# Moving the DRAM copies of queries and keys: four later places in the beginning, eight places in the middle stretch

## The chip, the cores and the metric

The kernel runs on one core of a Trainium2 chip. The metric is the device time of one launch in microseconds. A core has TensorE (PE; its weight loads are PEld), VectorE (DVE), ScalarE (ACT), GpSimd (POOL) and SyncE (SP). Each works through its own instructions in order. SP does nothing here but issue transfers; POOL issues some too. All transfers share 16 DMA engines.

## The reference, cut to what matters

Three layers follow one another. Attention looks back over a window of 64 positions; its 4 batches of 576 positions and 8 heads of 64 become 2304 tokens of width 512. A gated layer multiplies two products of the tokens. A mixture layer lets 32 slots collect the tokens, sends the slots through 8 experts and gives the result back to the tokens.

```python
scores = scale * np.matmul(q, k.transpose(0, 1, 3, 2))      # q, k, v: (4, 8, 576, 64)
mask = (rel >= 0) & (rel < 64)
attn = softmax(np.where(mask, scores, -1e9))
x = np.matmul(attn, v)                                      # as 2304 tokens x 512
x = (x @ w_a) * (x @ w_b) @ w_out                           # 512 -> 1536 -> 512
logits = x @ phi                                            # 32 slots
d = softmax(logits, over tokens); slot_input = d.T @ x
slot_out[e] = relu(slot_input[e] @ w1[e]) @ w2[e]           # 8 experts, 4 slots each
out = softmax(logits, over slots) @ slot_out
```

## The kernel before

The tokens are worked in 18 tiles of 128. For each tile attention makes scores (`att_s`), divides them by their sums (`att_n`), turns them (`att_pt`) and multiplies with the values (`att_pv`, tile `xps`). Then the gated layer (`glu`) makes three column groups of 512; each group is two products of 12 matmuls, in the PSUM banks `psa` and `psb`, and ACT copies `psa` out (L505) before the next `psa` may start. The products of the gated layer are then turned and multiplied with the projected slot weights (`r_b` and `r_l`), and the mixture layer's sums run along (`r_k`, `r_d`, `r_u`).

Much of the turning is done by way of DRAM. `r_b` turns 32x32 squares on DVE (`gq`), writes four pieces to DRAM (`gd`, L552) and reads them back in another order (`gT`, L557), all from SP's queue; `r_l` uses `gT` on TensorE (tile `lps` or `ups`, L573). From tile 7 on `att_pt` does the same with the scores from POOL's queue: `pq` on DVE, four writes `pd` (L374), two reads `pT` (L380), which `att_pv` needs.

Queries and keys of tiles 9 and up (`NTURN`) come turned as well: `relay_part` (L211) copies a quarter of one batch's queries or keys from the input to a DRAM tensor `dq` or `dk`, 2304 runs of 32 numbers, and `load_turned` (L205) reads from there. A batch's queries are four such copies, its keys another four. Batch 2 begins with tile 9, batch 3 in the middle of tile 13. So there are 16 copies, and all 16 are in the beginning.

The work has two stretches. The beginning, tiles 0 to 4 and parts of 5 and 6, follows the string `STARTUP`, in which each word is the next piece of one function; within it every engine's order is that of the string. `Xq2` is the next copy of batch 2's queries, `Xk3` the next of batch 3's keys. `Po` is a piece of `project_phi`, which reads and decodes `w_out` (L427 on ACT, L429 to L439 on DVE), turns it on TensorE (tile `two`) and writes it back from POOL (`wo_dram`, L701). `Sa`, `Sb`, `Da` and `Db` read and decode the gated layer's weights.

After that come slots 30 to 107, one slot for each product of the gated layer, with `events` that hang further work on a slot (`at(slot, function, ...)`). There only TensorE's order is that of the program. The order on the other engines, SP among them, is chosen when the program is compiled, by a planner that works with durations of its own; it may also take instructions of these slots ahead of the last words of `STARTUP`. Slot 46 holds `att_s` of tile 9 and `load` of tile 10's queries and keys, slot 64 the load of tile 13's.

Of the kernel before, what the change touches and what calls it, by code (L numbers as in the profile page):

```python
# [34 lines left out]
    Da1.1 Po1 Gb1.0 As3 Da1.1 Gb1.0 Po1 Gb1.0 Ga1.0 An3.0 Po1 Sb1.0 As4 Av2 As4 Ak5 Po1 Po1 Ga2.0 Sb1.1  # L35
    Sa1.0 An3.0 Da1.1 Gb1.0 Sb1.1 An3.1 An3.0 Po1 As4 Po1 Aq5 Da1.0 Ga2.0 Ga2.0 Ap3.1 Ap3.1 Tq5 Da1.1 Ap3.0 Tv3
    Da1.0 Da1.0 Po2 Ap3.0 Tv3 Db1.0 Ga2.0 Da1.0 Gb2.0 Ak5 Av3 Ak5 Da1.0 Gb2.0 Gb2.0 Av3 Av3 Gb2.0 Db1.0 Ga2.0
    Po2 Ga3.0 Ga3.0 Da1.0 As4 Ga3.0 Gb2.0 Ga3.0 Tq6 Xq2 Xk2 Da1.0 Aq6 Db1.0 Ga3.0 Tv4 Gb3.0 Ga0.1 As4 Db1.0
    Sa2.1 Po2 Ga0.1 Db1.0 Po2 Sa2.1 Tq6 Xq2 Xk2 Xq2 Ga0.1 Gb3.0 As4 Ga0.1 Db1.0 Po2 Po2 Po2 An4.0 An4.0
    An4.1 Tv4 As5 Db1.0 Ga0.1 Gb3.0 Po1 Po2 Sb2.0 Ga2.1 An4.0 Ga2.1 Po2 Gb3.0 Po4 Po2 As5 Po2 Gb3.0 Aq6  # L40
    Db1.1 Db1.1 Ga2.1 Po2 Db1.1 Ga2.1 Db1.1 Ap4.1 Po2 Ga2.1 Gb2.1 Ap4.1 Ap4.0 Po2 Ap4.0 Db1.1 Po4 Po2 Db1.1 Ga1.1
    Db1.1 Po4 Ga1.1 Po2 Sb2.0 Ga1.1 Po4 Po4 Gb2.1 Po4 Av4 Sa2.0 Ga1.1 Gb2.1 Ga1.1 Po2 Sa2.0 Da2.0 Gb2.1 Po4
    Gb2.1 Av4 As5 Ga3.1 Da2.0 Ga3.1 Po4 Da2.0 Da2.0 Av4 Po4 Po5 Ga3.1 Gb3.1 Gb3.1 Da2.0 Po4 Po4 Po4 Ga3.1
    As5 Po4 Ga3.1 Ak6 Gb3.1 Gb3.1 Po4 Gb3.1 Ak6 Po5 Da2.0 Ga4.1 Da2.0 Po4 Ga4.1 Po5 As5 Po4 Po5 Po4
    Po5 Ga4.1 Ga4.1 Gb1.1 Gb1.1 Po5 Ga4.1 Po5 Gb1.1 Ga4.0 Gb1.1 As5 Ga4.0 Da2.1 Ak6 Gb1.1 Da2.1 Ga4.0 Po5 Ga4.0
    Tv5 Po5 An5.0 Po5 An5.0 Gb4.0 Da2.1 Ga4.0 Da2.1 Gb4.0 Po5 Sb2.1 Gb4.0 Da2.1 Sb2.1 Da2.1 Po5 Gb4.0 Po5 Gb4.0
    Ga3.2 An5.0 Ga3.2 Po5 An5.1 Db2.1 Da2.1 Gb0.1 Gb0.1 Ap5.0 Db2.1 Ga3.2 Ga3.2 Db2.1 Db2.1 Ap5.1 Po5 Db2.1 Po5 Gb0.1
    Tv5 Xk2 Xq2 Xk2 Ga3.2 Ga2.2 Gb0.1 Gb0.1 Ap5.1 Db2.0 Ga2.2 Db2.1 Ga2.2 Db2.0 Ga2.2 Gb4.1 Db2.0 Db2.0 Gb4.1 Gb4.1
    Ap5.0 Ga2.2 Db2.0 Db2.1 Po3 Db2.0 Ga0.2 Po3 Xq3 Xk3 Xq3 Xk3 Ga0.2 Gb4.1 Ga0.2 Gb4.1 Po3 Ga0.2 Db2.0 Po3
    Av5 Po3 Gb2.2 Gb2.2 Gb2.2 Po3 Po3 Ga0.2 Ga4.2 Po5 Gb2.2 Gb2.2 Ga4.2 Po3 Po3 Po3 Ga4.2 Gb0.2 Po3 Po3  # L50
    Po3 Gb0.2 Gb0.2 Tv6 Ga4.2 Av5 Gb0.2 Ga4.2 Po3 Po3 Ga1.2 Gb0.2 Po3 Av5 Gb3.2 Gb3.2 Rt0.0 Gb3.2 Rt0.0 Gb3.2
    Rt0.1 Rt0.1 Rt0.2 Po3 Ga1.2 Rt0.2 Gb3.2 Gb4.2 Rl0 Gb4.2 Rl0 Rk0 Gb4.2 Rk0 Gb4.2 Ga1.2 Rk0 Rk0 Gb4.2 Rk0
    Ga1.2 Rk0 Ga1.2 Gb1.2 Rd0 Gb1.2 Gb1.2 Gb1.2 Rd0 Gb1.2 Tv6 Xq3 Xk3 Xq3 Xk3 Ru0 Ru0
"""
MANUAL = {mybir.EngineType.PE}
QUEUES = {mybir.EngineType.PE, mybir.EngineType.DVE, mybir.EngineType.Activation, mybir.EngineType.Pool, mybir.EngineType.SP}
# [8 lines left out]
def swa_glu_softmoe_kernel(  # L65
# [13 lines left out]
    nc = tc.nc  # L79
    B, H, S, D = q.shape  # L80
# [108 lines left out]
    def runs(t0, n):  # L189
        done = 0  # L190
        while done < n:
            b, s = divmod(t0 + done, S)
            step = min(n - done, S - s)
            yield done, step, b, s
            done += step
# [11 lines left out]
    def relay_part(nm, b, i, d):  # L207

        src = (q if nm == "q" else k)[b].rearrange("h s d -> (h s) d")
        n = H // 2 * S  # L210
        nc.sync.dma_start(  # L211
            out=d.rearrange("a (j e) -> a j e", e=32),
            in_=src[n * (i // 2):n * (i // 2) + n, 32 * (i % 2):32 * (i % 2) + 32].rearrange("(j a) e -> a j e", a=32),
        )

    def relay(nm, b):

        d = turned[nm, b] = dram.tile([4, 32, H // 2 * S], F32, name=f"d{nm}{b}")
        for i in range(4):
            relay_part(nm, b, i, d[i])  # L220
            yield

    def load(t, names="qkab"):
        tiles = loaded.setdefault(t, {})
        for nm, src, t0 in (("q", q, P * t), ("k", k, P * t), ("a", v, P * t - W), ("b", v, P * t)):
# [3 lines left out]
            o = 0  # L229
            if nm in "qk" and t >= NTURN:  # L230
                for off, n, b, s in runs(t0, P):
# [21 lines left out]
    def att_q(t):  # L253
        if t >= NTURN:
            x = loaded[t]["q"].rearrange("p h d -> p (h d)")
            nc.scalar.activation(out=x, in_=x, func=ACTF.Copy, scale=-SCALE)
            yield
            qT = qTs[:, t % 2]
            nc.vector.transpose(out=qT.rearrange("p u s -> p (u s)"), in_=x)
            sts[t] = {"qT": qT}  # L260
            return
        tq = ps_t.tile([P, 4, P], F32, tag="t", name="tq")
        x = loaded[t]["q"]
        for u in range(4):
            transpose(tq[:, u], x[:, 2 * u:2 * u + 2].rearrange("p h d -> p (h d)"))
        yield
        qT = qTs[:, t % 2]
        nc.scalar.activation(out=qT, in_=tq, func=ACTF.Copy, scale=-SCALE)
        sts[t] = {"qT": qT}

    def att_k(t):
# [5 lines left out]
        yield  # L277
        if t >= NTURN:
            x = loaded[t]["k"].rearrange("p h d -> p (h d)")
# [114 lines left out]
    def att_pv(t):  # L394
        st = sts[t]
        xps = ps_t.tile([P, 4, P], F32, tag="x", name="xps", bufs=1)
        for b in range(2):
            vt = loaded[t]["b" if b else "a"]
            c = slice(W * b, W * b + W)
            for n in range(H):  # L400
                h, u = divmod(n, 4) if t >= NTURN else (n % 2, n // 2)
                o = xps[W * (n % 2):W * (n % 2) + W, n // 2, c]
# [444 lines left out]
    def at(n, f, *a):  # L847
        events[round(4 * n) if n > NSLOT - 3 else 2 * round(2 * n)].append((f, a))
# [58 lines left out]
    a, b, c = LAST  # L907
# [203 lines left out]
    with tc.manual_schedule(engines=MANUAL | {mybir.EngineType.Activation, mybir.EngineType.DVE}):  # L1111
# [57 lines left out]
```

## Time and profile before

| | us |
|---|---|
| median of 3 runs | 526.72 |
| lowest, highest | 524.45, 527.68 |
| the profiled execution, device time | 524.64 |
| its span, first to last instruction | 522.7 |
| mean granted TensorE clock over the span | 0.973 |

The profiled execution has 1.94 us outside its span. TensorE is busy in 92% of the span, DVE in 58%, ACT in 37%. In timelines a line gives start, duration, engine, line of the kernel, operation, tile written and tiles read, how many, and in brackets how long the engine sat idle before and what ended that.

### The profile page before, as it was taken

What the parts mean: (1) busy time and instruction counts of PE and PEld (TensorE: products, weight loads), DVE (VectorE), ACT (ScalarE), POOL (GpSimd) and SP (SyncE); (2) the same over time, 40 slices, a digit from 0 to 9 for tenths busy, and PEclk for the clock granted to TensorE, in tenths of its full rate; (3) what the DMA queues carried; (4) which work ended last, traced back from release to release, by engine and by line L of the source; (5) the groups of instructions that cost most, each with busy time, mean ns of one, the idle gap of its engine ahead of it and who ended that gap; (6) DMA issues with size and microseconds to landing.
All of it is one profiled execution on the core that took longest, in us unless ns stands there. A gap on an engine that the chain in (4) does not pass through costs nothing.

```text
span 522.7 us, 10423 instructions
## 1 busy us (share of the span) xinstructions
PE 482.2 (92%) x3911; PEld 355.6 (68%) x3911; DVE 300.7 (58%) x759; ACT 193.1 (37%) x586; POOL 64.8 (12%) x136
## 2 busy tenths in 40 slices
PE   3769999999699969999999999999999999999993
PEld 2547777778477746777777777877777777743352
DVE  4989796896614543847667485677673211151133
ACT  4877765733421401324424143334432211231022
POOL 4101000000000020111130211212243000020000
PEclk9798999999799979999999999999999999999998
DMA  9999999589804186789877777875679999799998
GB/s 262 293 287 288 280 217 315 162 194 190 167 2 108 35 205 157 185 223 213 229 182 196 194 171 208 229 195 151 192 208 266 323 349 374 254 367 391 383 344 287
DMA packets 164898, 121.22 MB, mean 232 GB/s; under 512 B 102512, under 2 KB 141936, under 8 KB 164848
## 3 DMA queue, kind: packets, MB, share of 16 engines
q1 hardware_dynamic: 160112, 105.87, 72.1%
q0 software_dynamic: 4736, 14.68, 9.4%
q8 instruction: 31, 0.51, 0.4%
q14 instruction: 19, 0.16, 0.1%
HBM read 95.88 MB, written 29.36 MB: 240 GB/s over the span
## 4 chain that ended last, share of the span: by engine, by line
PE 70%; DMA 18%; ACT 4%; DVE 3%; SPq 2%; issue 1%; POOL 0%; DVEq 0%; POOLq 0%; ACTq 0%
PE psb L498 26%; PE psa L498 25%; DMA xw<-in_moe_w_dram 7%; PE xps L408 3%; PE ups L676 2%; DMA ldk<-in_k_dram 2%; PE s L317 2%; DMA ldb<-in_v_dram 2%; ACT pr L337 2%; DMA gd<-gq 2%; PE ups L573 1%; DMA st<-in_moe_w_out_dram 1%; PE tg L140 1%; PE two L140 1%; DMA pT<-pd 1%
## 5 line engine op out<-in xcount | busy, mean ns | idle before, releaser
L498 PE MATMUL psa<-wa,x 128*128 128x512 f32 x648 | 170.7, 405 | 5.8 <-ACT g L505 5.1
L498 PE MATMUL psb<-wb,x 128*128 128x512 f32 x648 | 169.0, 403 | 0.0
L498 PEld LDWEIGHTS psa<-wa,x 128*128 128x128 f32 x648 | 120.0, 192 | 33.8 <-ACT g L505 5.3
L498 PEld LDWEIGHTS psb<-wb,x 128*128 128x128 f32 x648 | 119.3, 191 | 27.6 <-issue 3.1
L510 DVE TENSOR_TENSOR g<-psb,g 128x512 f32<-128x512 f32 (+1 forms) x54 | 36.4, 676 | 62.9 <-PE psb L498 61.4
L505 ACT COPY g<-psa 128x512 f32<-128x512 f32 x53 | 30.9, 583 | 81.7 <-PE psa L498 75.7
L337 ACT ACTIVATE pr<-pr,nmx 128x128 f32<-128x128 f32 x96 | 37.2, 389 | 21.5 <-DVE nmx L330 21.5
L546 DVE STREAM_TRANSPOSE gq<-g 128x512 f32<-128x512 f32 x42 | 29.2, 703 | 8.0 <-DMA gd<-gq 7.4
L374 POOL DMA_DIRECT2D pd<-pq x44 | 24.2, 558 | 73.0 <-DVE pq L367 67.7
L358 DVE TENSOR_TENSOR pr<-pr,rs 128x512 f32<-128x512 f32 x36 | 24.4, 683 | 0.7
L609 ACT ACTIVATE e<-lt,nm 128x128 f32<-128x128 f32 x17 | 6.2, 365 | 49.7 <-DVE nm L605 46.9
L411 ACT CAST x<-xps 128x512 fp32r<-128x512 f32 x18 | 10.5, 585 | 37.2 <-PE xps L408 37.2
L276 POOL COPY kTs<-kTs 128x256 f32<-128x256 f32 x17 | 7.9, 463 | 122.8 <-DVE kTs L291 49.6
L317 PE MATMUL s<-kTs,qTs 64*64 64x128 f32 x576 | 21.9, 293 | 0.0
L330 DVE CUSTOM_DVE_ANT_0 pr<-s,masks 128x128 f32<-128x128 f32 x80 | 17.6, 285 | 7.1 <-PE s L317 7.1
L380 POOL DMA_DIRECT2D pT<-pd x22 | 16.5, 756 | 38.4 <-DMA pd<-pq 34.1
L317 PEld LDWEIGHTS s<-kTs,qTs 64*64 64x64 f32 x576 | 17.2, 144 | 5.8 <-issue 5.2
L337 ACT ACTIVATION_READ_ACCUMULATOR pr<-pr,nmx 128x1 f32 x96 | 17.9, 186 | 0.0
L337 ACT ACTIVATE pr<-s,nmx 128x128 f32<-128x128 f32 x48 | 17.0, 378 | 1.8 <-DVE nmx L327 1.8
L413 DVE TENSOR_TENSOR x<-xps,x 128x512 fp32r<-128x512 f32 x18 | 12.3, 685 | 8.9 <-ACT x L411 8.9
L701 POOL DMA_DIRECT2D wo_dram<-wo x6 | 4.5, 754 | 102.2 <-DVE wo L439 76.4
L427 ACT ACTIVATE w<-st 128x1024 f32<-128x1024 f32 (+1 forms) x14 | 14.3, 1023 | 7.2 <-DMA st<-in_moe_w_a_dram 3.8
(155 smaller groups left out, 602.3 us busy)
## 6 DMA issues: line engine op xcount, KB each, us to landing
xw<-in_moe_w_dram SPq DMA_DIRECT2D x46, 512.0 KB, 6.6
gd<-gq SPq DMA_DIRECT2D x168, 64.0 KB, 2.9
gT<-gd SPq DMA_DIRECT2D x42, 256.0 KB, 3.1
xw<-in_moe_w_dram SPq DMA_DIRECT2D x27, 256.0 KB, 7.2
st<-in_moe_w_b_dram SPq DMA_DIRECT2D x12, 512.0 KB, 6.1
st<-in_moe_w_out_dram SPq DMA_DIRECT2D x12, 512.0 KB, 5.5
st<-in_moe_w_a_dram SPq DMA_DIRECT2D x12, 512.0 KB, 7.2
pd<-pq POOLq DMA_DIRECT2D x44, 128.0 KB, 3.5
```

The source lines that it names most:

```text
L317: nc.tensor.matmul(sps[h][c, u], lhsT=qT[r, u, c], rhs=kTs[r, t % 2, u, W * b:W * b + P], start=not early, stop=not early or u == 3,)
L330: nc.vector.tensor_tensor_reduce(out=pr[:, u].rearrange("p (a k) -> p a k", a=2), in0=sps[h][:, u].rearrange("p (a k) -> p a k", a=2), in1 ...
L337: nc.scalar.activation(out=pr[:, u], in_=sps[h][:, u] if early else pr[:, u], func=ACTF.Exp, scale=-1.0, bias=nmx[:, i:i + 1], accum_out=s ...
L358: nc.vector.tensor_tensor(out=pr, in0=pr, in1=rs.to_broadcast([P, 4, P]), op=ALU.mult)
L374: nc.gpsimd.dma_start(out=pd[:, :, i].rearrange("j k e -> k j e"), in_=pq[32 * i:32 * i + 32].rearrange("p j h u q -> p j (h u q)"),)
L380: nc.gpsimd.dma_start(out=pT, in_=pd[:, :, :, P * h:P * h + P].rearrange("j k i e -> (j k) i e"))
L408: nc.tensor.matmul(o, lhsT=vt[:, n, :], rhs=r)
L427: nc.scalar.activation(out=t, in_=hi.bitcast(F32), func=ACTF.Abs)
L498: nc.tensor.matmul(ps, lhsT=l[:, kk], rhs=r, start=(n == 0), stop=(n == 3 * KD - 1))
L505: nc.scalar.copy(out=pas[t, fg], in_=ps)
L510: nc.vector.tensor_tensor(out=g[:, c:c + step], in0=ps[:, c:c + step], in1=pa[:, c:c + step], op=ALU.mult)
L546: nc.vector.transpose(out=gq.rearrange("p (j c t) -> p c j t", j=4, c=4), in_=gts[t][:, 512 * fg:512 * fg + 512].rearrange("p (c j f) -> p ...
```

## The change

Nothing that is computed changes, and there are 16 copies as before. In `STARTUP` the first pair of copies is taken out, the next three words are batch 2's first three (`Xq2 Xk2 Xq2`), of the next three words one is left (`Xk2`), the four words that copied batch 3 copy the rest of batch 2, and the four words at the end are taken out. Batch 3's eight copies hang on slots 46, 48, ... 60, queries and keys in turn. Each is put directly behind the SP instruction that was traced last before it (`keep_in_program_order`).

```diff
-... Ga3.0 Tq6 Xq2 Xk2 Da1.0 Aq6 Db1.0 ...
+... Ga3.0 Tq6 Da1.0 Aq6 Db1.0 ...
 ... Sa2.1 Tq6 Xq2 Xk2 Xq2 Ga0.1 ...
-... Tv5 Xk2 Xq2 Xk2 Ga3.2 ...
+... Tv5 Xk2 Ga3.2 ...
-... Db2.0 Ga0.2 Po3 Xq3 Xk3 Xq3 Xk3 Ga0.2 ...
+... Db2.0 Ga0.2 Po3 Xq2 Xk2 Xq2 Xk2 Ga0.2 ...
-... Gb1.2 Tv6 Xq3 Xk3 Xq3 Xk3 Ru0 Ru0
+... Gb1.2 Tv6 Ru0 Ru0
+    LATER = 46
-        nc.sync.dma_start(
+        return nc.sync.dma_start(
         for i in range(4):
-            relay_part(nm, b, i, d[i])
-            yield
+            yield relay_part(nm, b, i, d[i])
+    relays = {}
+    def relay_late(nm, b):
+        if (nm, b) not in relays:
+            relays[nm, b] = relay(nm, b)
+        tc.keep_in_program_order(next(relays[nm, b]))
+    for n in range(8):
+        at(LATER + 2 * n, relay_late, "qk"[n % 2], B - 1)
```

## Rows read from the trace of the kernel before

**Rows 1.** The page, part 1: engine, busy us, share of the span, instructions.
```profile
PE 482.2 (92%) x3911; PEld 355.6 (68%) x3911; DVE 300.7 (58%) x759; ACT 193.1 (37%) x586; POOL 64.8 (12%) x136
```

**Rows 2.** Windows: from:to, length, busy us by engine (instructions), PEclk, DMA share, GB/s.
```profile
20.00:59.00 39.00, 32.72 (x354) 24.24 (x351) 35.74 (x54) 29.28 (x83) 2.34 (x4) 0.96 1.07 290
59.00:131.00 72.00, 70.93 (x488) 55.23 (x491) 58.13 (x70) 38.57 (x81) 3.00 (x5) 1.00 0.89 221
130.00:163.00 33.00, 27.92 (x189) 21.09 (x187) 13.87 (x41) 10.59 (x33) 0.72 (x1) 0.90 0.40 78
177.00:201.00 24.00, 16.59 (x138) 11.99 (x135) 12.03 (x42) 5.96 (x24) 3.72 (x6) 0.86 0.66 155
234.00:292.00 58.00, 57.42 (x506) 44.28 (x502) 39.64 (x139) 20.68 (x82) 11.31 (x19) 1.00 0.83 205
```

**Rows 3.** Timeline of SP: three of the 16 copies, and tile 13's queries.
```profile
60.91 3.41 SPq L211 DMA_DIRECT2D dk<-in_k_dram  x1
...
119.84 0.55 SPq L211 DMA_DIRECT2D dq<-in_q_dram  x1
...
135.38 1.88 SPq L211 DMA_DIRECT2D dk<-in_k_dram  x1
...
297.95 1.21 SPq L205 DMA_DIRECT2D ldq<-dq  x2
```

**Rows 4.** DMA from 134 to 138 us, when copies alone were in flight.
```profile
DMA packets 4927, 0.63 MB, mean 156 GB/s; under 512 B 4927, under 2 KB 4927, under 8 KB 4927
```

**Rows 5.** Timeline of TensorE: its idle times from 59 to 190 us.
```profile
92.24 0.66 PE L140 MATMUL two<-ident,wo 128*128 128x128 f32 x4 [1.07 <-DVE wo L439]
...
130.91 1.10 PE L317 MATMUL s<-kTs,qTs 64*64 64x128 f32 x32
137.10 1.65 PE L498 MATMUL psa<-wa,x 128*128 128x512 f32 x3 [5.08 <-ACT g L505]
...
186.12 0.49 PE L593 MATMUL lt<-l,ri 128*128 128x128 f32 x2 [4.14 <-DVE l L583]
```

**Rows 6.** Timeline of ACT: what stands ahead of two copies TensorE waits for.
```profile
87.08 1.13 ACT L427 ACTIVATE wo<-st 128x1024 f32<-128x1024 f32 x1 [2.40 <-DMA st<-in_moe_w_out_dram]
...
132.38 0.40 ACT L337 ACTIVATE pr<-pr,nmx 128x128 f32<-128x128 f32 x1 [6.64 <-DVE nmx L330]
...
135.47 1.10 ACT L427 ACTIVATE wo<-st 128x1024 f32<-128x1024 f32 x1
136.48 0.56 ACT L505 COPY g<-psa 128x512 f32<-128x512 f32 x1
```

**Rows 7.** Timeline of POOL: the reads of turned scores, tiles 9, 10 and 11.
```profile
248.56 1.50 POOL L380 DMA_DIRECT2D pT<-pd  x2 [3.30 <-DMA pd<-pq]
...
271.31 1.50 POOL L380 DMA_DIRECT2D pT<-pd  x2 [3.61 <-DMA pd<-pq]
...
293.28 1.50 POOL L380 DMA_DIRECT2D pT<-pd  x2 [3.46 <-DMA pd<-pq]
```

**Rows 8.** Timeline of TensorE: where those reads and `gT` are used.
```profile
255.33 0.69 PE L408 MATMUL xps<-pT,lda 128*64 128x64 f32 x16
...
261.07 0.84 PE L573 MATMUL ups<-gT,wphi 128*32 128x128 f32 x24
...
277.98 0.69 PE L408 MATMUL xps<-pT,lda 128*64 128x64 f32 x16
...
300.08 0.69 PE L408 MATMUL xps<-pT,lda 128*64 128x64 f32 x16
```

**Rows 9.** Landing: of `pT`, 234 to 300; issues with KB and median, 234 to 292.
```profile
DMA to landing us min/median/max: 3.6/4.2/4.7
...
gT<-gd SPq DMA_DIRECT2D x12, 256.0 KB, 3.1
gd<-gq SPq DMA_DIRECT2D x48, 64.0 KB, 3.0
```

**Rows 10.** Timeline of SP: the last `gT` read of tile 6.
```profile
253.89 0.34 SPq L557 DMA_DIRECT2D gT<-gd  x1
```

**Rows 11.** Issues by tile, median landing: 106 to 113 us, then 140.8 to 146.
```profile
wo_dram<-wo POOLq DMA_DIRECT2D x1, 512.0 KB, 7.0
...
wo_dram<-wo POOLq DMA_DIRECT2D x1, 512.0 KB, 4.5
```

More of the change, by code (lines that the diff above doesn't have):

```diff
@@ L37 @@
     Da1.0 Da1.0 Po2 Ap3.0 Tv3 Db1.0 Ga2.0 Da1.0 Gb2.0 Ak5 Av3 Ak5 Da1.0 Gb2.0 Gb2.0 Av3 Av3 Gb2.0 Db1.0 Ga2.0
[L38 to L51, printed above, removed]
@@ L52 @@
-    Rt0.1 Rt0.1 Rt0.2 Po3 Ga1.2 Rt0.2 Gb3.2 Gb4.2 Rl0 Gb4.2 Rl0 Rk0 Gb4.2 Rk0 Gb4.2 Ga1.2 Rk0 Rk0 Gb4.2 Rk0
-    Ga1.2 Rk0 Ga1.2 Gb1.2 Rd0 Gb1.2 Gb1.2 Gb1.2 Rd0 Gb1.2 Tv6 Xq3 Xk3 Xq3 Xk3 Ru0 Ru0
+    Po2 Ga3.0 Ga3.0 Da1.0 As4 Ga3.0 Gb2.0 Ga3.0 Tq6 Da1.0 Aq6 Db1.0 Ga3.0 Tv4 Gb3.0 Ga0.1 As4 Db1.0 Sa2.1 Po2
+    Ga0.1 Db1.0 Po2 Sa2.1 Tq6 Xq2 Xk2 Xq2 Ga0.1 Gb3.0 As4 Ga0.1 Db1.0 Po2 Po2 Po2 An4.0 An4.0 An4.1 Tv4
+    As5 Db1.0 Ga0.1 Gb3.0 Po1 Po2 Sb2.0 Ga2.1 An4.0 Ga2.1 Po2 Gb3.0 Po4 Po2 As5 Po2 Gb3.0 Aq6 Db1.1 Db1.1
@@ new lines @@
+    Ga2.1 Po2 Db1.1 Ga2.1 Db1.1 Ap4.1 Po2 Ga2.1 Gb2.1 Ap4.1 Ap4.0 Po2 Ap4.0 Db1.1 Po4 Po2 Db1.1 Ga1.1 Db1.1 Po4
+    Ga1.1 Po2 Sb2.0 Ga1.1 Po4 Po4 Gb2.1 Po4 Av4 Sa2.0 Ga1.1 Gb2.1 Ga1.1 Po2 Sa2.0 Da2.0 Gb2.1 Po4 Gb2.1 Av4
+    As5 Ga3.1 Da2.0 Ga3.1 Po4 Da2.0 Da2.0 Av4 Po4 Po5 Ga3.1 Gb3.1 Gb3.1 Da2.0 Po4 Po4 Po4 Ga3.1 As5 Po4
+    Ga3.1 Ak6 Gb3.1 Gb3.1 Po4 Gb3.1 Ak6 Po5 Da2.0 Ga4.1 Da2.0 Po4 Ga4.1 Po5 As5 Po4 Po5 Po4 Po5 Ga4.1
+    Ga4.1 Gb1.1 Gb1.1 Po5 Ga4.1 Po5 Gb1.1 Ga4.0 Gb1.1 As5 Ga4.0 Da2.1 Ak6 Gb1.1 Da2.1 Ga4.0 Po5 Ga4.0 Tv5 Po5
@@ new lines @@
+    An5.0 Po5 An5.0 Gb4.0 Da2.1 Ga4.0 Da2.1 Gb4.0 Po5 Sb2.1 Gb4.0 Da2.1 Sb2.1 Da2.1 Po5 Gb4.0 Po5 Gb4.0 Ga3.2 An5.0
+    Ga3.2 Po5 An5.1 Db2.1 Da2.1 Gb0.1 Gb0.1 Ap5.0 Db2.1 Ga3.2 Ga3.2 Db2.1 Db2.1 Ap5.1 Po5 Db2.1 Po5 Gb0.1 Tv5 Xk2
+    Ga3.2 Ga2.2 Gb0.1 Gb0.1 Ap5.1 Db2.0 Ga2.2 Db2.1 Ga2.2 Db2.0 Ga2.2 Gb4.1 Db2.0 Db2.0 Gb4.1 Gb4.1 Ap5.0 Ga2.2 Db2.0 Db2.1
+    Po3 Db2.0 Ga0.2 Po3 Xq2 Xk2 Xq2 Xk2 Ga0.2 Gb4.1 Ga0.2 Gb4.1 Po3 Ga0.2 Db2.0 Po3 Av5 Po3 Gb2.2 Gb2.2
+    Gb2.2 Po3 Po3 Ga0.2 Ga4.2 Po5 Gb2.2 Gb2.2 Ga4.2 Po3 Po3 Po3 Ga4.2 Gb0.2 Po3 Po3 Po3 Gb0.2 Gb0.2 Tv6
@@ L54 @@
+    Ga4.2 Av5 Gb0.2 Ga4.2 Po3 Po3 Ga1.2 Gb0.2 Po3 Av5 Gb3.2 Gb3.2 Rt0.0 Gb3.2 Rt0.0 Gb3.2 Rt0.1 Rt0.1 Rt0.2 Po3
+    Ga1.2 Rt0.2 Gb3.2 Gb4.2 Rl0 Gb4.2 Rl0 Rk0 Gb4.2 Rk0 Gb4.2 Ga1.2 Rk0 Rk0 Gb4.2 Rk0 Ga1.2 Rk0 Ga1.2 Gb1.2
+    Rd0 Gb1.2 Gb1.2 Gb1.2 Rd0 Gb1.2 Tv6 Ru0 Ru0
 """
```

## The prediction, made before the changed kernel was run

> **What bounds the kernel now.** The page comes first: TensorE is busy in 92% of the span [rows 1], so a change pays only where TensorE waits. The copies are issued by SP from about 60 us to 137 us [rows 3], so I read the windows of that stretch and of the slots that receive the copies [rows 2]. From 59 to 131 us TensorE is busy 70.93 of 72 us at full clock. The DMA engines have a share of 0.89 there and look like the bound; they aren't. From 234 to 292 us TensorE is busy 57.42 of 58 us, and the DMA share is already 0.83. In the full stretch from 20 to 59 us it reached 1.07, which I take as the ceiling (a share is the sum of packet times, and packets overlap).
>
> Next I looked for TensorE's idle times in its timeline. From 59 to 190 us three are over 1 us [rows 5]: 1.07 us ahead of 92.24, 5.08 ahead of 137.10, 4.14 ahead of 186.12. The last two come with a lower granted clock: the window from 130 to 163 has 0.90, the one from 177 to 201 has 0.86, so part of each ran at 1.2 GHz instead of 2.4 [rows 2]. The reader should see that the copies are near these holes in time and still end none of them. ACT's timeline says what does [rows 6]: the copy of `psa` at 136.48 stands behind eight exponentials that began at 132.38, after ACT had sat idle 6.64 us for scores that TensorE made at 130.91 [rows 5]. These scores are tile 6's, from slot 30: the planner took them ahead of the last words of the beginning. A DMA counts only for the first hole: the decoding at 87.08 waited 2.40 us for `w_out` [rows 6].
>
> **The price of one copy.** From 134 to 138 us copies alone were in flight. They moved 4927 packets; a copy is 2304 runs, so that is 2.14 copies in 4.00 us, or 1.87 us of all 16 engines each [rows 4]. SP is held for 0.55 us where the queue is empty, 1.88 behind other copies, 3.41 behind other loads [rows 3].
>
> **The beginning loses eight copies.** That is 8 x 1.87 = 15.0 us of the engines, and nearly all of it lies beside a TensorE that is busy anyway. What can be gained is in the 1.07 us ahead of 92.24. `w_out` can land a little sooner because two of the five copies before 76 us are gone; it can't be issued much sooner, since its one staging buffer has to be free first. Bounds: 0 and -1.1; I take half, -0.5. The four copies at the end ran beside the 5.08 us hole, but the hole waits for ACT's order and not for a transfer, so I book nothing; the work that hides them is TensorE's and ACT's own. If that cover were gone, all eight are worth their 15.0 us.
>
> **Batch 2's copies in other places.** Three stay where they were with other contents, one of three stays near 107 us, four stay near 120 us. The first load that reads them is tile 9's, which hangs on slot 40, two tiles before the 255.33 us of slot 52 [rows 8]. Nothing: the slack is tens of us.
>
> **The middle gains eight copies.** `xps` of tiles 9, 10 and 11 hangs on slots 52, 58 and 64 and runs at 255.33, 277.98 and 300.08 [rows 8], so six slots take 22.4 us, slot 46 begins at about 233 and slot 60 at about 285; with what stands ahead of them on SP the copies fall between 234 and 292. The engines' room: 0.83 of 58 us is 48.1; at the ceiling of 1.07 that needs 45.0 us, so 13.0 are free, and 15.0 come. That is 2.0 us too many. At a ceiling of 1.00 it is 9.9 free and 5.1 too many. So the stretch becomes full, and transfers wait for each other. Who waits for whom:
>
> Behind a copy on SP stand the `gd` writes and the `gT` read of the next group. `gT` of tile 6's last group was issued at 253.89 [rows 10], lands 3.1 later [rows 9], and is used from 261.07 on, last group about 0.4 us later [rows 8]: slack 4.5 us. `gd` takes 3.0 and `gT` cannot be issued before it has landed, so each copy that comes between costs this loop up to 1.87 us. Four copies (slots 46 to 52) lie ahead, up to 7.5 us.
>
> POOL's loop is tighter. The second read `pT` of tile 9 is issued half-way through 248.56 to 250.06, at 249.31 [rows 7], lands 4.2 later [rows 9], and TensorE uses it at 255.33 [rows 8]: slack 1.8 us. Tiles 10 and 11 give 1.7 and 1.8 by the same sum (272.06 and 294.03; used at 277.98 and 300.08). Behind a late `pT` the scores of the next tile and all further products stand on TensorE.
>
> How much a POOL transfer suffers from copies is seen in `wo_dram`: 4.5 us alone, 7.0 us with copies and loads of SP beside it [rows 11], 2.5 us more on 512 KB. A leg of `pd` or `pT` (512 KB each over all pieces) should suffer no more than that, and by one copy at most 1.87.
>
> The Trainium skill, "DMA: Bandwidth & Descriptors", section "Queues, rings and completion order", says that a DMA engine takes turns between the queues it has work for, packet by packet, while one queue's own work is taken in order. By that rule POOL's legs would lose only a part of a copy's 1.87 us and SP's `gd` the whole, and the sum would be near the lower end below; the 2.5 us [rows 11] show that the legs lose something and don't tell the shares.
>
> Bounds for the middle: 0 us if the slacks of 4.5 and 1.8 us take everything, and 15.0 if nothing is hidden. The nearest rows are the two for the engines' room, 2.0 and 5.1. I take 3.0, because a part of the 5.1 goes into `gT`'s slack. No clock is lost: single waits of 1 or 2 us did not lower it (the 1.07 us hole lies in a window with 1.00).
>
> **One thing later.** Tile 13's load, issued at 297.95 [rows 3], reads batch 3, whose last copy hangs on slot 60, near 285. It has some 12 us, less what SP has ahead of it, to be issued and to land. If the copies are late, SP waits at this load with the next `gd` behind it; this is part of the range, not of the sum.
>
> **The sum.** 524.64 - 0.5 + 0 + 3.0 = 527.1 for an execution like the profiled one. That execution was 2.1 us under the median of 526.72. For the median I predict 526.7 + 2.5 = 529.2.
>
> **The rivals.**
> A, the forecast, chance 0.34: the middle is full, and slacks take part of it. 526.7 - 0.5 + (0.8 to 5.8) = 527 to 532.
>
> B, chance 0.29, slower: the loops by way of DRAM become the bound. Each of tiles 9 to 11 meets a copy on both legs: 6 x 1.87 = 11.2, less slacks of 5.3, is 5.9 us; SP's loop adds what its 7.5 us exceed the slack of 4.5, some 3.0, in between. About 8.9 - 0.5 = +8.4, so 535; without SP's part 532. For it: slack 1.8 us [rows 7 to 9]. Against it: a wait of TensorE gives the other loop time. A rule of the Trainium skill stands behind B ("DMA: Bandwidth & Descriptors", section "Latency and other measured facts": DRAM takes much longer to answer under high load); no row here separates DRAM's answer from waiting in a queue.
>
> C, chance 0.27, the other side, faster: the planner, which times transfers by its own durations, finds the end of the beginning less full and no longer takes tile 6's scores ahead. Place: the hole ahead of 137.10. Price: 5.08 us of idle [rows 5] and up to 0.10 x 33 = 3.3 us of clock in that window [rows 2], about 7.5 together. It decides if the copy of `psa` (L505) stands ahead of tile 6's exponentials on ACT. With the middle at +3.0 that is 521.7, with a hidden middle 518.7. The second hole, 24 - 16.59 = 7.4 us of idle [rows 2], could go with it. Against it: that hole waits for DVE's order, which a transfer may not touch.
>
> D, chance 0.10: everything is hidden, in the middle too: 526.2. For it: the slack of `gT` and TensorE's own 57.42 of 58. The rule on turns above leans this way.
>
> **Chances and range.** This kernel's measurement tells about 1% from no change, so the bounds are 521.5 and 532.0. A and D are within 1%, and so is a quarter of C: 0.34 + 0.10 + 0.07 and 0.01 of B, 0.52. Faster: 0.20, from C. Slower: 0.28, from B. The range takes in C with a middle of nothing and B with both parts, 519 to 536; A alone is 527 to 532.
>
> **What would show it.** The eight L211 issues between 234 and 295 us; the DMA share from 234 to 292 near 1.0 (A, B) or still under 0.95 (D); TensorE idle ahead of `xps` by `pT`, or ahead of L573 by `gT`, 3 us in all (A), 6 and more (B), none (D). From 59 to 131 us TensorE as full as before. The hole ahead of L498 near 137 us: there (A, B, D) or gone (C). I am wrong in the mechanism if the beginning gains more than 1.1 us ahead of 131 us, or if time moves in places that no copy touches, since the planner's order elsewhere may shift too.

## The result: 513.8 us, and where the profile shows it

| | before | after |
|---|---|---|
| median of 6 runs, us | 526.73 | 513.78 |
| lowest, highest | 524.45, 527.68 | 512.54, 515.03 |
| span of the profiled execution | 522.7 | 511.9 |

The ratio is 0.9758, with a 95% interval of 0.9733 to 0.9783: 2.4% faster, and below the predicted range. (Ratios leave out runs more than 1.5% above the fastest of their kernel, medians and ranges take in all.) The instructions on TensorE are the same, and in the same order but for 32: the scores of tile 6 run at 130.91 us before and at 152.89 after. Both places lie between `xps` of tiles 5 and 6, so the timeline can be cut at the first matmul of `xps` of each tile, and each stretch compared with itself. (In the changed kernel most lines stand 8 lower: L498 is now L506, L557 is L565.)

| from `xps` of tile | before | after | difference |
|---|---|---|---|
| start to 5 | 127.57 | 126.21 | -1.36 |
| 5 to 6 | 48.49 | 40.63 | -7.86 |
| 6 to 7 | 34.56 | 23.41 | -11.15 |
| 7 to 9 | 44.71 | 44.75 | +0.04 |
| 9 to 10 | 22.65 | 29.06 | +6.41 |
| 10 to 11 | 22.10 | 22.10 | 0 |
| 11 to 12 | 20.99 | 24.75 | +3.76 |
| 12 to the end | 201.64 | 200.95 | -0.69 |

So 20.4 us were won ahead of tile 7, 10.2 lost in the middle, and the rest hardly moved: -10.85 us in all. (The medians differ by 12.95; before's profiled execution was 2.1 us under its median.) The first row is uncertain: traces of kernels with the changed kernel's beginning take 124.01 (thin) to 127.65 us (e3) there, and kernels with every copy at its old place 127.57 to 129.28 (f3_bp). The -7.86 and the -11.15 are far outside what the same stretches scatter in kernels of the same order. The page's first part and windows of the changed kernel, with the columns of [rows 1] and the columns and stretches of [rows 2]:

```profile
PE 479.0 (94%) x3911; PEld 353.3 (69%) x3911; DVE 299.4 (58%) x759; ACT 193.2 (38%) x586; POOL 64.8 (13%) x136
```

```profile
20.00:59.00 39.00, 33.36 (x350) 24.83 (x351) 35.98 (x54) 29.79 (x83) 2.69 (x5) 0.95 1.07 296
59.00:131.00 72.00, 72.00 (x491) 56.64 (x490) 61.68 (x74) 40.34 (x84) 3.09 (x6) 1.00 0.78 204
130.00:163.00 33.00, 33.00 (x227) 25.73 (x226) 14.51 (x44) 10.57 (x33) 0.72 (x1) 1.00 0.32 80
177.00:201.00 24.00, 24.00 (x216) 18.50 (x215) 15.81 (x50) 7.46 (x27) 5.33 (x11) 1.00 0.75 192
234.00:292.00 58.00, 53.46 (x476) 40.33 (x478) 35.23 (x123) 18.20 (x74) 8.21 (x14) 0.97 0.84 194
```

All three idle times of [rows 5] are gone, with their lowered clock. In the middle TensorE is busy 53.46 us in place of 57.42, while the DMA share of this window rose by 0.01 only. (The changed kernel runs 20 us ahead here and issued the eight copies from 214 to 281 us; over the 69 us from 214 on the share is 0.87, against 0.82 in the kernel before from 234 on.) Timeline of TensorE there, its waits and two ends of stretches:

```profile
235.01 0.69 PE L416 MATMUL xps<-pT,lda 128*64 128x64 f32 x16
...
256.13 0.42 PE L581 MATMUL ups<-gT,wphi 128*32 128x128 f32 x8 [1.23 <-DMA gT<-gd]
259.23 0.43 PE L581 MATMUL ups<-gT,wphi 128*32 128x128 f32 x8 [2.67 <-DMA gT<-gd]
259.59 4.55 PE L506 MATMUL psb<-wb,x 128*128 128x512 f32 x12
...
264.07 0.69 PE L416 MATMUL xps<-pT,lda 128*64 128x64 f32 x16
...
294.14 0.43 PE L581 MATMUL ups<-gT,wphi 128*32 128x128 f32 x8 [1.61 <-DMA gT<-gd]
302.37 3.02 PE L506 MATMUL psb<-wb,x 128*128 128x512 f32 x12 [1.67 <-DVE g L518]
```

Every wait of the first stretch is for `gT`, none for `pT`. The waits make 3.90 of the 6.41 us. Of the rest, 1.53 us are clock: twelve products `psb` behind the waits took 4.55 us, against 3.02 at 302.37.

### The profile page after: what moved, and what is told of

It reads as the page before. It is cut to its first block, busy times and chain, and to the rows that moved or that the text cites. A ratio compares the mean times of both kernels' runs of the same rounds, so it can differ in the third digit from the quotient of the medians.

```text
span 511.9 us, 10433 instructions
## 1 busy us (share of the span) xinstructions
PE 479.0 (94%) x3911; PEld 353.3 (69%) x3911; DVE 299.4 (58%) x759; ACT 193.2 (38%) x586; POOL 64.8 (13%) x136
## 4 chain that ended last, share of the span: by engine, by line
PE 76%; DMA 14%; DVE 3%; SPq 3%; ACT 2%; issue 1%; DVEq 0%
PE psb L506 28%; PE psa L506 26%; DMA xw<-in_moe_w_dram 7%; PE xps L416 4%; PE s L325 3%; PE ups L684 2%; DMA gd<-gq 2%; DMA ldb<-in_v_dram 2%; DMA gT<-gd 1%; PE ups L581 1%; PE tg L141 1%; PE two L141 1%; PE tp L141 1%; PE lps L581 1%; DMA ldk<-dk 1%
## 5 line engine op out<-in xcount | busy, mean ns | idle before, releaser
L506 PE MATMUL psb<-wb,x 128*128 128x512 f32 x648 | 168.8, 402 | 2.5 <-DVE g L518 1.7
L506 PE MATMUL psa<-wa,x 128*128 128x512 f32 x648 | 168.0, 400 | 0.7 <-DVE wa L490 0.7
L506 PEld LDWEIGHTS psb<-wb,x 128*128 128x128 f32 x648 | 118.7, 190 | 30.7 <-issue 2.9
L506 PEld LDWEIGHTS psa<-wa,x 128*128 128x128 f32 x648 | 118.1, 189 | 27.5 <-issue 3.4
L581 PE MATMUL ups<-gT,wphi 128*32 128x128 f32 x312 | 11.5, 274 | 5.5 <-DMA gT<-gd 5.5
```

The source lines that it names most:

```text
L506: nc.tensor.matmul(ps, lhsT=l[:, kk], rhs=r, start=(n == 0), stop=(n == 3 * KD - 1))
L581: nc.tensor.matmul(lps[32 * i:32 * i + 32].rearrange("p (i t) -> p i t", t=32) if t in by_squares else lps[32 * i:32 * i + 32], lhsT=wphi[ ...
```

## The experiments

The questions are three: what closed the first hole (5 to 6), what closed the second (6 to 7), and why the middle cost three times what was booked. ORDER stands for the order in which the scheduler put instructions on ACT and DVE, TRAFFIC for the copies as transfers. Medians are of 4 runs unless said; the kernel before ran beside them, at 526.3 to 527.7.

### The first hole

One pin in the kernel before; no copy moves:

```diff
-                    nc.tensor.matmul(
+                    mm = nc.tensor.matmul(
 ...
+                    if t == NFIRST + 1 and (u, h, b) == (0, 0, 0):
+                        tc.keep_in_program_order(mm)
```

> The kernel before, with all 16 copies at their old places. One line is added: the first matmul of tile 6's scores is put directly behind the TensorE instruction traced before it, so the planner can't take these scores ahead of the beginning's last words. Orders on SP and POOL are word for word those of before. Theory ORDER (the planner's order at the joint of the two stretches made the gain, the copies' transfers in the beginning cost nothing): the hole ahead of 137 us goes, 5.1 us of idle and about 2.4 of clock, so 519 us; if the hole at 177 to 201 goes with it, 509. Theory TRAFFIC (the copies' transfers and their time on SP held the beginning up): no gain, 526 to 527.

Measured: 521.37 us (517.82 to 521.86), ratio 0.9852 [0.978, 0.9924]; 5 to 6 takes 40.63 us, the changed kernel's number to the last digit. The second hole stays and grows, from 34.56 to 37.90 us, which hides 3.3 us of the gain in the whole. The other way round, tile 6's scores put ahead by hand in the changed kernel:

```diff
-... Gb2.2 Gb2.2 Gb2.2 Po3 Po3 Ga0.2 ...
+... Gb2.2 Gb2.2 Gb2.2 As6 As6 As6 As6 As6 As6 Po3 Po3 Ga0.2 ...
-        at(s, att_s, t)
+        if t > NFIRST + 1:
+            at(s, att_s, t)
```

> The changed kernel, but tile 6's scores are written into the string of the beginning at the place where the planner took them in the kernel before (behind the third Gb2.2, in six words As6). Orders on SP and POOL are those of the changed kernel. ORDER: the hole comes back, about 7.5 us, 521 us. TRAFFIC: 513 to 514.

Measured: 520.77 us (516.05 to 526.9; the median is 518.26 without the longest run), ratio 0.9833 [0.9745, 0.9922]; 5 to 6 takes 46.54, so 5.9 of the 7.86 us are back. ACT's timeline of this kernel, then TensorE's:

```profile
129.40 0.40 ACT L345 ACTIVATE pr<-pr,nmx 128x128 f32<-128x128 f32 x1 [5.49 <-DVE nmx L338]
...
132.11 0.39 ACT L345 ACTIVATE pr<-pr,nmx 128x128 f32<-128x128 f32 x1
132.50 0.56 ACT L513 COPY g<-psa 128x512 f32<-128x512 f32 x1
```

```profile
133.11 0.95 PE L506 MATMUL psa<-wa,x 128*128 128x512 f32 x3 [4.08 <-ACT g L513]
```

That is [rows 6] again: eight exponentials, the copy of `psa` behind them, TensorE idle for it. In the changed kernel, where tile 6's scores come at 152.89, ACT has this order:

```profile
124.41 1.13 ACT L435 ACTIVATE wo<-st 128x1024 f32<-128x1024 f32 x1
126.32 0.58 ACT L513 COPY g<-psa 128x512 f32<-128x512 f32 x1 [0.78 <-PE psa L506]
```

Which of the moved words decides? Two of them alone:

```diff
-... Tv5 Xk2 Xq2 Xk2 Ga3.2 ...
+... Tv5 Xk2 Ga3.2 ...
-... Po3 Xq3 Xk3 Xq3 Xk3 Ga0.2 ...
+... Po3 Xq2 Xk2 Xq3 Xk3 Ga0.2 ...
-... Tv6 Xq3 Xk3 Xq3 Xk3 Ru0 Ru0
+... Tv6 Xq3 Xk3 Xq3 Xk3 Xq3 Xk3 Ru0 Ru0
```

> Edit: before, with only the two copies that stand behind Tv5 in the third group taken from there and put with the last four (the copies of batch 2 first). Nothing is left out. ORDER: these two words alone decide whether the scheduler takes tile 6's scores ahead, so the first hole closes (tile 5 to 6: 48.49 to 40.6 us) and the second stays as in e1 and e2 (34 to 38): 518 to 522 us. TRAFFIC: 2 of 16 copies move, each 1.87 us of the DMA engines: within 2 us of before's 526.7, with the first hole at 46 to 49 us.

Measured: 519.74 us (519.1 to 521.12), ratio 0.987 [0.9833, 0.9907]; 5 to 6 takes 40.63, 6 to 7 takes 34.11. Tile 6's scores now stand where e1 and the changed kernel have them, behind the start-up, as TensorE's timeline of only_third shows:

```profile
154.84 1.10 PE L325 MATMUL s<-kTs,qTs 64*64 64x128 f32 x32
```

So two copies behind `Tv5` decide the first hole, by where the scheduler then puts tile 6's scores. Why its plan turns on these two isn't in the traces.

### The second hole

Kernels that end the start-up with copies have it (before, e1, only_third); the changed kernel doesn't. All of batch 3's copies to the end:

```diff
-    Rd0 Gb1.2 Gb1.2 Gb1.2 Rd0 Gb1.2 Tv6 Ru0 Ru0
+    Rd0 Gb1.2 Gb1.2 Gb1.2 Rd0 Gb1.2 Tv6 Ru0 Ru0 Xq3 Xk3 Xq3 Xk3 Xq3 Xk3 Xq3 Xk3
-    for n in range(8):
-        at(LATER + 2 * n, relay_late, "qk"[n % 2], B - 1)
```

> The changed kernel's beginning, but batch 3's eight copies stand at the end of the string and none in the middle. PE, DVE, ACT and POOL have the order of e1; only SP's differs, in the copies' places. ORDER: the same as e1 within 1.5 us. TRAFFIC: 4 us and more below e1, because two copies fewer stand ahead of 75 us and two fewer at 107 us.

Measured: 519.43 us (517.51 to 520.95), ratio 0.9836 [0.9778, 0.9894]; 6 to 7 takes 34.57, the four stretches from 8 to 12 take 22.6, 23.1, 22.1 and 21.0. The hole is back and the middle's loss is gone. The whole is 1.94 us below e1, between what ORDER and what TRAFFIC gave, so this run leaves open which of them makes the hole. DVE's timeline of e1 (before with the first pin) shows an order, then TensorE's of the same stretch:

```profile
174.00 0.69 DVE L360 TENSOR_TENSOR pr<-pr,rs 128x512 f32<-128x512 f32 x1
...
177.10 1.85 DVE L548 STREAM_TRANSPOSE gq<-g 128x512 f32<-128x512 f32 x3
178.88 0.25 DVE L585 COPY l<-lps 128x128 f32<-128x128 f32 x1
```

```profile
172.03 3.02 PE L500 MATMUL psa<-wa,x 128*128 128x512 f32 x12
179.18 0.80 PE L595 MATMUL lt<-l,ri 128*128 128x128 f32 x2 [4.14 <-DVE l L585]
...
186.29 0.33 PE L140 MATMUL dps<-ident,e 128*128 128x128 f32 x1 [2.06 <-ACT ce L645]
...
194.31 0.65 PE L575 MATMUL ups<-gT,wphi 128*32 128x128 f32 x8 [3.71 <-DMA gT<-gd]
```

The small copy `l`, which TensorE waits for, stands behind tile 7's scores and three transposes `gq` of earlier tiles. These transposes could have run before. So DVE's order alone was changed, with every copy at its old place. The first reduction of `att_s` of tile 7 has to stand behind two `gq` of tile 2, and the first addition of its `att_n` behind `l` of tile 1 and the third `gq`:

```diff
+                if t == NPLAIN and i == 0:
+                    for key in ((2, 0), (2, 1)):
+                        tc.add_manual_dep(red.ins, turn_ins[key].ins.name, ...)
 ...
+            if t == NPLAIN and hh == 0:
+                for key in ((1, "l"), (2, 2)):
+                    tc.add_manual_dep(add.ins, turn_ins[key].ins.name, ...)
```

> Edit: before, with every copy at its old place, and the engines' order pinned at two places. The first matmul of tile 6's scores is pinned as in the run before (e1_before_pin6, 521.4 us), and now VectorE has to take the gq transposes of tiles 2 and 3 and the small copy l ahead of the first reductions and additions of tile 7's scores. No copy moves, nothing is left out. ORDER says that the second hole (tile 6 to 7: 37.90 us in e1, 23.41 in after) is only this order on VectorE: the stretch falls to 23.4 to 25 us, the whole to 505 to 512 us, and so below the changed kernel's 513.8 without moving a copy. TRAFFIC says that the hole comes from four copies queued behind one another at the end of the start-up: nothing of this is taken away here, so the stretch stays at 34 to 38 us and the time at 518 to 522.

Measured: 512.31 us (511.95 to 513.15), ratio 0.9728 [0.9687, 0.9768]. 6 to 7 fell from 37.90 to 28.34 us. The same pins on e2:

> Edit: the changed kernel with batch 3's eight copies at the end of the start-up in place of the middle stretch (e2_b3_at_end, 519.4 us), and the same two pins on VectorE as in f2_bp. Nothing is left out. ORDER: tile 6 to 7 falls from 34.57 to 23.4 to 25 us, and since no copy stands in the middle the whole comes to 503.5 to 510 us, close to the kernel without batch 3's copies (503.7). TRAFFIC: eight copies in a row on SP's queue hold the loads of gT behind them: the stretch stays at 32 us or more and the time at 517 to 520.

Measured: 510.7 us (509.67 to 511.55), ratio 0.9694 [0.9658, 0.9729]; 6 to 7 takes 28.70. ORDER has the larger part of the hole in both, but neither stretch came down to its 23.4 to 25, and both times lie just above its ranges. What was left on TensorE in f2_bp:

```profile
176.17 0.49 PE L608 MATMUL lt<-l,ri 128*128 128x128 f32 x2 [0.35 <-DVE l L598]
182.21 0.48 PE L140 MATMUL dps<-ident,e 128*128 128x128 f32 x1 [2.59 <-ACT ce L658]
```

`ce` waits for a reduction on DVE that stands behind tile 7's multiplications; a third pin put both of them behind tile 1's `nm`, and `att_n` of tile 7 half a slot later:

```diff
+        if t == NPLAIN:
+            tc.add_manual_dep(mul.ins, turn_ins[1, "nm"].ins.name, ...)
-        at(s + 1, att_n, t, 0)
+        n1 = s + (1.5 if t == NPLAIN else 1)
+        at(n1, att_n, t, 0)
```

> Edit: f2_end (510.7 us) with one more pin on VectorE. In f2_end TensorE still idled 2.59 us ahead of dps at 180.73 us, and the next psa took 4.59 us in place of 2.99, since VectorE took tile 7's four multiplications and transposes of scores ahead of the small reduction tm of tile 1 that ce, and with it dps, waits for. Now those multiplications stand behind tile 1's nm. Nothing is left out. ORDER: the stretch from tile 6 to 7 falls from 28.70 to the 23.4 us of the changed kernel, and the whole to 503.5 to 507 us, below the changed kernel (513.8). TRAFFIC (the rest of the hole comes from the eight copies in a row): it stays at 28 us and the time at 509 to 512.

Measured: 510.18 us (507.48 to 511.8), ratio 0.9687 [0.9628, 0.9747]; 6 to 7 takes 26.20.

> Edit: f2_bp (512.3 us; every copy at its old place, two pins) with the same third pin as in f3_end. Nothing is left out. ORDER: tile 6 to 7 falls from 28.34 to 23.4 us and the whole to 505.5 to 509 us: the changed kernel's whole gain, and more, without moving a copy. TRAFFIC: 28 us and 511 to 514 stay.

Measured: 510.82 us (510.37 to 513.06), ratio 0.9713 [0.9659, 0.9768]; 6 to 7 takes 26.20. Both miss what ORDER gave (503.5 to 507, and 505.5 to 509): the wait for `ce` shrank, and `gT` took its place, as the timeline of f3_end shows:

```profile
178.79 0.33 PE L141 MATMUL dps<-ident,e 128*128 128x128 f32 x1 [0.44 <-ACT ce L669]
184.52 0.43 PE L599 MATMUL ups<-gT,wphi 128*32 128x128 f32 x8 [1.43 <-DMA gT<-gd]
```

In another execution of f3_end the stretch took 28.24, with 2.11 us ahead of that `ups`, so the third pin's gain is within the scatter. Of the second hole in e1, 14.5 us over the changed kernel's 23.41, the pins on DVE took 9.6 to 11.7; the rest is mainly waits for `gT`, and whether copies or order make those isn't separated.

### The middle

Batch 3's copies left out altogether:

```diff
-        d = turned[nm, b]
+        d = turned[nm, min(b, B - 2)]
-    for n in range(8):
-        at(LATER + 2 * n, relay_late, "qk"[n % 2], B - 1)
```

> The changed kernel without batch 3's eight copies; the loads of batch 3 read batch 2's copies instead, so batch 3's queries and keys are left out of the computation. It prices the eight copies in the middle. If they cost what TensorE idles there in the changed kernel (1.23 + 2.67 + 1.61 us ahead of L581, 1.67 ahead of L506, some clock): 505 to 508 us. If the middle hides them: 513 to 514.

Measured: 503.72 us (503.39 to 507.57), ratio 0.9557 [0.9495, 0.9619]; 9 to 10 takes 22.65, 11 to 12 takes 20.99. All 10.2 us are the copies', and the whole is a little below the 505 to 508 that were expected. Next, copies at the same slots with few bytes:

```diff
+        m = 128 if b == B - 1 else n
 ...
-            out=d.rearrange("a (j e) -> a j e", e=32),
+            out=d[:, 0:m].rearrange("a (j e) -> a j e", e=32),
```

> Edit: the changed kernel with each of batch 3's eight copies cut to 128 of 2304 positions, at the same eight places of the middle; batch 3's loads then read the copies of batch 2, so batch 3's own queries and keys are left out. TRAFFIC in the middle: the 10.2 us that tiles 9 to 12 lost are the bytes of the copies among the loads of the loop on SP's queue: the stretches 9 to 10 and 11 to 12 fall back to 22.7 and 21.0 us and the whole to 503.5 to 506. PLACES: the loss is the eight instructions' place ahead of gT's loads on SP, whatever they carry: the stretches stay near 29 and 25 us and the whole at 511 to 514.

Measured: 507.3 us (502.43 to 508.42), ratio 0.9612 [0.9555, 0.9669]; the stretches are 22.65 and 20.99 again; the whole is a little above TRAFFIC's 506. It is what the copies carry, not the eight instructions. (The edit cuts bytes and runs together; which of the two counts isn't separated.) SP shows how. Up to 240 us SP has the same instructions in the same order in both kernels. First the changed kernel, from one `gT` of tile 4 to the first of tile 7, then thin:

```profile
199.06 0.34 SPq L565 DMA_DIRECT2D gT<-gd  x1
...
214.19 0.63 SPq L212 DMA_DIRECT2D dq<-in_q_dram  x1
215.16 3.19 SPq L565 DMA_DIRECT2D gT<-gd  x1
...
225.08 1.12 SPq L212 DMA_DIRECT2D dk<-in_k_dram  x1
226.25 5.03 SPq L560 DMA_DIRECT2D gd<-gq  x4
...
243.92 0.34 SPq L565 DMA_DIRECT2D gT<-gd  x1
```

```profile
195.99 0.34 SPq L566 DMA_DIRECT2D gT<-gd  x1
...
210.03 0.63 SPq L213 DMA_DIRECT2D dq<-in_q_dram  x1
211.07 0.35 SPq L566 DMA_DIRECT2D gT<-gd  x1
...
219.64 0.60 SPq L213 DMA_DIRECT2D dk<-in_k_dram  x1
220.28 2.88 SPq L561 DMA_DIRECT2D gd<-gq  x4
...
234.72 0.46 SPq L566 DMA_DIRECT2D gT<-gd  x1
```

The copy itself holds SP 0.6 to 1.1 us. What is issued behind it is held: `gT` for 3.19 us against 0.35, four `gd` for 5.03 against 2.88. (Not every issue is: seven `gd` from 220.43 on took 3.72 us, against 5.41 in thin.) The chain takes 44.86 us against 38.73, 6.13 more. Three copies lie in it, at 214.19, 225.08 and 236.29; the fourth is issued at 244.31, behind its end. 1.09 of the 6.13 us are there before the first copy. From the first copy on it is 29.73 us against 24.69, so each copy puts the chain back by 1.68 us, near the 1.87 us of engines in [rows 4]. (The expectations below have 1.5, counted with four copies.)

The DMA engines were not full over the whole stretch, but nearly so in parts of it. These are the windows just ahead of TensorE's waits, of the changed kernel and then of about the same work in thin:

```profile
244.00:254.00 10.00, 9.65 (x48) 7.46 (x50) 6.30 (x17) 1.56 (x7) 3.43 (x6) 1.00 0.97 223
```

```profile
240.00:250.00 10.00, 10.00 (x48) 8.24 (x47) 6.90 (x19) 1.49 (x6) 3.22 (x6) 1.00 0.69 173
```

So it isn't separated whether an issue behind a copy is held by its place in SP's queue or by engines that are busy at that moment.

Does it help to spread the copies, every 4 slots from 32 on or every 3 from 40 on? The edit of the first:

```diff
-    LATER = 46
+    LATER = 32
-        at(LATER + 2 * n, relay_late, "qk"[n % 2], B - 1)
+        at(LATER + 4 * n, relay_late, "qk"[n % 2], B - 1)
```

> Edit: the changed kernel with batch 3's eight copies on slots 32, 36, ... 60 in place of 46, 48, ... 60; all copies are whole and nothing is left out. LOOP says that each copy puts the loop of gd and gT on SP's queue 1.5 us back (44.86 us in the changed kernel and 38.73 in thin for the same instructions from 199.06 and 195.99 us on, over four copies) and that the loop wins time back where it is not disturbed: at half the density nothing of the 10.2 us should be left in the stretches 9 to 10 and 11 to 12, and the whole is 503.5 to 507 us. BYTES says that eight copies cost their transfer wherever they stand among the loads: 511 to 514. The order on VectorE that the scheduler makes differs from the changed kernel's from the scores of tile 7 on; a hole at that place would be that order's, not the copies'.

> Edit: the same on slots 40, 43, ... 61: between the changed kernel (every 2 slots) and sp32_4 (every 4). Nothing is left out. Up to tile 8 the order on VectorE and ScalarE is that of the changed kernel. LOOP: a copy every 3 slots leaves part of the reserve: the two stretches together lose 0 to 4 us, the whole 504 to 508 us. BYTES: 511 to 514.

Measured: 513.96 us (508.2 to 517.83), ratio 0.9728 [0.9645, 0.981], and 517.13 us (513.43 to 521.92), ratio 0.9801 [0.9722, 0.988]; without the longest run of each the medians are 513.81 and 515.0. LOOP's numbers are missed in both. In their traces, which are of those longest runs, 9 to 10 takes 30.12 and 30.11 us and 11 to 12 is back at 20.99 and 21.97; in sp32_4, 7 to 8 takes 25.00. From tile 7 to 12 they lose 9.8 and 8.8 us, so half the density moved the loss and took little off it. Two reasons were left: the loop is behind from the start-up and has nothing to win back from, or a copy costs its transfer anywhere. Four of the eight copies went back to the end of the start-up of f3_end, and the other four to early slots, or to 54, 56, 58 and 60:

```diff
-... Tv6 Ru0 Ru0 Xq3 Xk3 Xq3 Xk3 Xq3 Xk3 Xq3 Xk3
+... Tv6 Ru0 Ru0 Xq3 Xk3 Xq3 Xk3
+    for n, s in enumerate((34, 37, 40, 43)):
+        at(s, relay_late, "qk"[n % 2], B - 1)
```

> Edit: f3_end with only the first four of batch 3's copies at the end of the start-up; the other four hang on slots 34, 37, 40 and 43 (about 170 to 215 us). All copies are whole, nothing is left out. BACKLOG (a copy among the slots costs TensorE something only while the loop of gd and gT is still behind from the start-up: in the changed kernel the square of tile 6's first group is ready at 206.6 us and written at 220.4): four copies at 1.5 us each use up the 5 to 6 us of slack that gT of each tile's last group has, and waits for gT appear up to tile 10: tiles 7 to 10 lose 2 to 8 us, the whole is 511 to 517. PLACELESS (each copy costs its transfer wherever it stands): the same 511 to 517. NEITHER (the order on VectorE made the loss in sp32_4, not the copies): 507 to 510.

> Edit: the same with the four copies on slots 54, 56, 58 and 60 (about 243 to 265 us). BACKLOG: the loop has caught up by then (in thin the square of tile 8's last group is ready at 249.1 and written at 250.4), so the 5 us of slack at each tile's last group take the copies: tiles 7 to 10 lose nothing, tiles 10 to 12 at most 1.5 us, the whole is 506.5 to 510. PLACELESS: four times 1.5 us, 511 to 517, as in half_early.

Measured, of 6 runs: early 517.57 us (513.45 to 520.44), ratio 0.9808 [0.9768, 0.9848]; late 516.76 us (513.0 to 520.12), ratio 0.9805 [0.9761, 0.9848]. Early loses in 7 to 8, which takes 29.44 us against 22.65 in f3_end; late loses in 11 to 12, 24.72 against 20.99. Both times TensorE waits for `gT`, here early and then late:

```profile
204.57 0.66 PE L597 MATMUL ups<-gT,wphi 128*32 128x128 f32 x8 [4.04 <-DMA gT<-gd]
```

```profile
292.83 0.43 PE L597 MATMUL ups<-gT,wphi 128*32 128x128 f32 x8 [2.17 <-DMA gT<-gd]
300.46 3.02 PE L521 MATMUL psb<-wb,x 128*128 128x512 f32 x12 [1.06 <-DVE g L533]
```

BACKLOG has the place right (0.4 us are lost from tile 7 to 10 in half_late) and the size wrong: it allowed 1.5 us behind tile 10, and 3.73 were lost. PLACELESS's 511 to 517 holds for the late median and is just missed by the early one, but the late trace lost 3.73 us and not four times 1.5. So a copy among the slots cost 0.9 us (late), 1.7 (early) and 1.3 in the changed kernel. The place of the copies alone doesn't set it: e4 has the changed kernel's copies in the same order on SP, and from tile 9 to 12 it lost 4.7 us, 0.6 each (25.18, 23.75 and 21.48 us). There TensorE had lost 5.9 us in the start-up, which left the chain that much more time. This fits BACKLOG, and it is one trace.

What isn't explained is that half_late's median lies 6.3 us above that of f3_end, while its profiled execution, one of its shortest, shows a loss of 3.73 in one stretch. Some time is lost behind tile 12 too, where no copy is in flight any more: in e4 TensorE waited 1.58 us for `pT` of tile 13, in the changed kernel's second trace 2.79 and 1.24. What makes that `pT` late wasn't tested.

### A version measured below both

> No edit: the changed kernel again, beside the others on the same chip. Every theory: 512.5 to 515.

> No edit: f3_end again (510.2 us), beside the changed kernel on the same chip. ORDER: 508 to 511, and below the changed kernel by 2 to 6 us. If its lead was the chip's: within 1 us of it.

Side by side, of 6 runs each: the changed kernel, a little above what every theory gave, 515.85 us (509.42 to 520.0; the median is 515.0 without its two longest runs), ratio 0.9743 [0.9696, 0.9791]; f3_end again 510.43 us (507.28 to 513.17), ratio 0.9676 [0.9643, 0.971]. The medians differ by 5.4 us (4.6 without those two runs), and the two intervals against before overlap by 0.0014, so the lead isn't clear of the noise in these runs alone. Both times f3_end was measured, its median lay under both of the changed kernel's (510.2 and 510.4 against 513.8 and 515.9).

## Why the prediction was wrong

**What bounds the kernel** was read rightly: TensorE's idle times, and no copy at their ends. Nearly all that was won is these idle times and the clock in them.

**The beginning**, -0.5 with bounds 0 and -1.1, measured -1.36: the 1.07 us ahead of 92.24 are gone in the changed kernel's trace. But this is one pair of traces, and the scatter of this stretch is larger. In e1, with every copy at its old place, the wait is gone as well; in f2_bp, also with old places, it is 1.84. No run shows which value between 0 and -1.1 the copies are worth here.

**The hole ahead of 137.10, booked at nothing: the step that failed.** The working takes the four copies beside the hole, says that it "waits for ACT's order and not for a transfer", and books no gain. The first half is true, and the conclusion doesn't follow, for the order is made by a scheduler that plans these very transfers: 7.86 us went with it. The copies that decide aren't those beside the hole, either. With six copies at the end the hole is closed (only_third); two copies behind `Tv5`, some 20 us earlier, had made it. The text knew the order's part as rival C, at 0.27. C's mechanism, place and sign (the copy of `psa` ahead of the exponentials) are what happened, and its price of 7.5 us is near the 7.86 measured. (Its two terms, 5.08 and up to 3.3, give up to 8.4; why 7.5 was taken isn't said.)

**The second hole**, 7.4 us of idle, was left out of C's price, because it "waits for DVE's order, which a transfer may not touch". A transfer's place does touch it: the hole is there in the kernels with copies at the end of the start-up (before, e1, e2, only_third) and not in those without (the changed kernel, e3, thin), and f2_bp took 9.6 us out of e1's by order alone. Its size was too small as well, 11.15 us, since only idle was counted and not the clock of 0.86 in the same row.

**The middle**, +3.0, measured +10.2. The sum was the engines' room: 13.0 free, 15.0 come. This term was mis-sized, because an average over 58 us doesn't show where the time goes. The share over the copies' own 69 us is 0.87 and far from the ceiling of 1.07; single windows reach 0.97. What sets the end is a chain on SP, write `gd`, wait until it has landed, read `gT`, and each copy in it puts it back by 1.68 us. Rival B had this chain with up to 1.87 us a copy, four copies, 7.5 us, less a slack of 4.5; the 1.68 over three copies bears the first number out. B's other half, POOL's `pT`, fell: no wait of tiles 9 to 11 is for `pT`. And "no clock is lost" fell: after 1.23 and 2.67 us of wait close together the next products ran at a lower clock. The Trainium skill's rule that an engine takes turns between queues ("DMA: Bandwidth & Descriptors", "Queues, rings and completion order") would fit a POOL that loses less than SP. No run here separates it from `pT`'s later need.

**The rivals were priced as if they shut each other out.** C is about the start-up, B about the middle; both came true. The prediction's own terms together, 526.7 - 0.5 - 7.5 - 7.4 + 8.9, give 520.2; with the second hole's clock (3.8 us more) and the beginning's -1.36 it is 515.5, near what was measured. (That sum was made after the result, with two of its terms measured.) The last paragraph had named the case, "time moves in places that no copy touches", and gave it no chance.

**The indicator** of DMA share (near 1.0 for A and B, under 0.95 for D) would have called D, with 0.84 from 234 to 292 us. The window was fixed in the time of the kernel before; by then the changed kernel had issued its first two copies. TensorE's wait for `gT`, 5.5 us in all, pointed between A and B.

## What to carry to other kernels

Where a compiler's scheduler orders instructions, a moved transfer can change the order of engines it never touches: look first at idle times that wait for order, give the chance that they go a term of its own, and add it to the rival about the new place. Pinning the order in the kernel before gave as large a gain without moving a transfer (f2_bp, 512.3 us, against 513.8), and it kept the freedom to put the transfers where nothing waits. Free room on the DMA engines, averaged over a stretch, says little about a chain that issues, waits for the landing and issues again: count the transfers that come between its links.

## What the runs showed that was not expected

An issue on SP behind one copy of 2304 short runs was held 3.19 us, against 0.35 behind a thin one, while the issue of the copy itself took 0.63 in both. Here the time shows on the instruction behind the copy, and not on the copy. And TensorE's granted clock, at 1.00 in the windows before, fell after the waits of 1.23 and 2.67 us:

```profile
256.00:265.00 9.00, 6.20 (x59) 4.57 (x60) 2.21 (x4) 0.00 (x0) 0.00 (x0) 0.81 0.81 166
```

This window of the changed kernel holds the second wait and the products behind it; at 0.81 a part of it ran at 1.2 GHz.
